# Empty rows written behind the counted tokens, another order in the ramp, operands placed by address modulo 256, and the tokens of expert 1 ahead of its weights' splits

## The chip, the cores and the metric

One core of one Trainium2 chip runs the whole program. The metric is the device time in microseconds (us); a lower time is better. The engines are called as the profile calls them: PE (TensorE, with PEld for its weight loads), DVE (VectorE), ACT (ScalarE), POOL (GpSimd), SP (SyncE, which here only issues DMAs).

## What is computed

Attention with a decaying state feeds a mixture of experts. Shapes: batch 4, 8 heads, 768 steps, head size 48; so 3072 tokens of width 384; 8 experts with 1024 hidden values.

```python
f = 1.0 / (1.0 + np.exp(-f_logit))
for t in range(S):
    state = f[:, :, t, :, None] * state + np.einsum('bhd,bhe->bhde', k[:, :, t], v[:, :, t])
    y[:, :, t] = np.einsum('bhd,bhde->bhe', q[:, :, t], state)
x = y.transpose(0, 2, 1, 3).reshape(B * S, H * D)
logits = x @ w_gate
e_idx = np.argmax(logits, axis=1)          # one expert per token
for e in range(E):
    mask = e_idx == e
    h = np.maximum(x[mask] @ w1[e], 0.0)
    out[mask] = gate_w[mask, None] * eom[mask, e, None] * (h @ w2[e])
```

## The kernel before

**Attention (L131 to L582).** The work is cut into 24 steps t: 4 batches (b) of 6 chunks (c) of 128 tokens. `prep` (L192) makes what step t needs from the raw inputs: `s` and `f` are sigmoids on ACT, `scan_p` and `scan_i` are running products on DVE, `mul_q` multiplies q by p on POOL, `mul_k` multiplies k by i on `eng` (DVE for t below 3 and from 22 on, else POOL, L196), `ends` copies the last column on ACT. The main loop (L462 to L546) calls them two steps ahead through `pre`, which does each only once. On PE a step is `qk(t)` (products of q and k, L249), `kn_tr(t)` (L266), `x_tr(t - 2)` (L326), `out_y(t - 1)` (L309, L313) and `state(t - 1)` (L282). `mask(t, par)` (L252) takes the two halves of the product out of PSUM: one half by an ACT copy and a POOL select, the other by one DVE multiplication; at t = 0 both go by ACT and POOL. `evac_y` (L320) and `evac_kn` are ACT copies that `x_tr` and `state` need.

**Order.** The order in which the program is written is the order on each of PE, ACT, DVE and POOL (`chain`, L1153), so an operation that waits holds everything written behind it on its engine. SP issues DMAs in the written order; eight of its DMAs are in flight, and the ninth waits for the first. `load` (L172) brings q, k, f, v; the loads of batches 2 and 3 are written in the loop at every third step, in the order f, k, q, v (L535).

**Routing.** Every few steps `route` and `slots` count the tokens of each expert; `scatter` (L337) writes each token's row (384 values, token number, logits: 401 values, 1604 bytes) to its slot in `xs_dram`, which has 3072 slots for each of the 8 experts. An expert's matmuls run over a fixed number of slots (`CAPS`: 512, 448, 432, 416, 400, 400, 384, 376, the fullest expert first), so slots behind the last token must hold empty rows with a token number too large to be written out. `clear(e)` (L664), called for all experts ahead of the loop (L434), fills the slots 256 to 511 of every expert with such rows: eight DMAs of 401 KB on SP's queue, behind the loads of batches 0 and 1. The expert with most tokens after step 15 is expert 0 in the order (`top`, L393); its first 256 tokens are read early (`tokens_in`), the rest after the last scatter; `find_order` (L911) then sorts the others.

**Experts (L945 to L1014).** Each value is split into a high and a low part (fp32r), and every product is made of three matmuls. For expert s: `split` cuts the weights (ACT copy, DVE subtraction), `x_in` (L767) turns the tokens by a DVE transpose (`xc`) and splits them (`xh` on ACT, `xl` on DVE), `mm1` (L798) makes 8 blocks f of 9 matmuls into one of two PSUM tiles `h_ps`, which ACT (`hh`, L813) and DVE (`hl`, L814) take out, and then come `mm2` (L828, tokens as the moving operand) for experts 1 to 5 or `mm2_row` (L838, w2 as the moving operand, 384 columns) for experts 0, 6 and 7. Expert 0's first 256 tokens have their own tiles (`xah`, `xal`, and hidden tiles in the pool `ha`), and run through `mm1` before the late tokens arrive; `x_late` (L757) turns the late ones. `gain` steps (L734 to L748, 13 per expert) make the factor of each token. During expert 0's last `mm2_row`s, `beside` (L991) pops at every second call one piece of a list `front` (here: split, tokens 0, split, tokens 1, tokens 2 of expert 1) and at the others one gain step of expert 1.

**Addresses.** A tile's place follows from the sizes allocated ahead of it in its pool. In bytes modulo 256 the program puts `xh`, `xl` and `hh`, `hl` of all late parts at 128, the weights' parts `w1h` to `w2l` at 224, and `xah`, `xal` and the tiles of `ha` at 224.

Of the kernel before, what the change touches and what calls it, by code (L numbers as in the profile page):

```python
# [21 lines left out]
C = 128  # L22
# [26 lines left out]
BW = DM // (128 // SB)  # L49

# [68 lines left out]
class Routing:  # L119


    def __init__(self, pool):
        self.pend = pool.tile([128, NTC * NP], F32, name="pend")

        self.ohb = pool.tile([128, len(RG) + 1, 5, E], BF16, name="ohb")
        self.slot = pool.tile([128, NTC], I32, name="slot")
        self.top = pool.tile([128, E], F32, name="top")
        self.top_id = pool.tile([128, 1], I32, name="top_id")


def attention(ctx, tc, nc, k, kpool, rt, q01, k01, f01, q23, k23, f23, v, wg, xs_dram, r, ex):  # L131
# [60 lines left out]
    def prep(ti):  # L192
# [3 lines left out]
        eng = nc.vector if ti < 3 or ti >= T_VEC else nc.gpsimd  # L196
# [55 lines left out]
    def mask(t, par):  # L252
        if t == 0 or par:
# [83 lines left out]
    def scatter(n):  # L337

        for _ in range(min(n, len(sq))):
# [7 lines left out]
            for other in ex.apart + (ex.cleared if (t + 1) * C <= HELD else []):  # L347
# [56 lines left out]

    def slots(gi, t0, n):
# [8 lines left out]
        if t0 + n == T_TOP:  # L414
            nc.tensor.matmul(cnt_ps, k.ones, r.ohb[:, gi + 1, 0, :], start=True, stop=True, skip_group_check=True)
            top(cnt_ps)
        rk = rt.tile([128, n, E], F32, name="rk")
        nc.vector.tensor_tensor(out=rk, in0=ps, in1=oh, op=ALU.mult)
        with nc.allow_low_precision(reason="one of the summands is not zero"):
            nc.vector.tensor_reduce(out=r.slot[:, ts], in_=rk, axis=AX.X, op=ALU.add)  # L420
        sq.extend(range(t0, t0 + n))
# [11 lines left out]
    for e in range(E):  # L433
        ex.clear(e)  # L434
# [29 lines left out]
    for t in range(last + 1):  # L464
# [6 lines left out]
        if t not in (0, 2):  # L471
# [4 lines left out]
        if t == 2:  # L476
            pre(4, "f")
# [7 lines left out]
        if t > 1 and not late:  # L485
# [18 lines left out]
        pre(t + 2, "mul_q", "ends")  # L504
# [7 lines left out]
        pre(t + 3, "s")  # L512
# [58 lines left out]
    drain()  # L571
    scatter(len(sq))
    ex.tokens_in(0, EARLY // TS, NT)
    ex.mm1_early(3)
    ex.find_order(two[:, 340:340 + E])
# [7 lines left out]
class Experts:  # L583
# [4 lines left out]
    def __init__(self, tc, nc, k, r, raw, right, w1, w2, xs_dram, out, kp, yd):  # L588
        self.tc, self.nc, self.k, self.r, self.raw, self.right, self.kp = tc, nc, k, r, raw, right, kp
        self.yd = yd  # L590
        self.w1, self.w2, self.xs, self.out = w1, w2, xs_dram.rearrange("(e n) w -> e n w", e=E), out
        k.gain = kp.tile([128, SLOTS // SB, E], F32, name="gain")
        k.dst = kp.tile([TS, NT, E], I32, name="dst")
        kp.tile([128, 8], F32, name="pad")

        self.first = kp.tile([TS, NT, RW], F32, name="first_x")
        self.apart, self.cleared, self.results, self.number = [], [], [], {}
        self.wr, self.whl, self.todo, self.gq, self.who = {}, {}, [], [], {}
        self.xg, self.xb, self.xt, self.hs, self.ys, self.ysb = {}, {}, {}, {}, {}, {}
# [11 lines left out]
    def open_rest(self, ctx):  # L611
        pool = lambda name, bufs, **kw: ctx.enter_context(self.tc.tile_pool(name=name, bufs=bufs, **kw))
        self.xp, self.hp, self.yp = pool("mo_x", 2), pool("mo_h", 9), pool("mo_y", 1)
# [50 lines left out]
    def clear(self, e):  # L664

        if e == 0:
            self.empty = self.kp.tile([TS, RW], F32, name="empty")
            self.nc.gpsimd.memset(self.empty, 0.0)
            self.nc.gpsimd.memset(self.empty[:, DM:DM + 1], float(BIG))
        n = (SLOTS - HELD) // TS  # L670
        i = self.nc.sync.dma_start(out=self.xs[e, HELD:SLOTS].rearrange("(j p) w -> p j w", p=TS),
                                   in_=self.empty.unsqueeze(1).broadcast_to([TS, n, RW]))
        self.cleared.append(i)
# [86 lines left out]
    def x_split(self, pool, c, ps, n, width, name):  # L760
        hi = pool.tile([128, width], F32R, name=f"{name}h{c}")
        lo = pool.tile([128, width], F32R, name=f"{name}l{c}")
# [4 lines left out]
    def x_in(self, s, c):  # L767
# [3 lines left out]
        x = self.xp.tile([128, SLOTS], F32, name="xc")  # L771
        self.nc.vector.transpose(out=x[:, 0:n].rearrange("p (a t) -> p a t", t=SB), in_=t[:, :, c::KC])
        self.xt[s, c] = self.x_split(self.xp, c, x[:, 0:CAPS[s]], CAPS[s], WIDE, "x")
# [459 lines left out]
```

## Time and profile before

| | us |
|---|---|
| median of 3 runs | 358.79 (358.48 to 359.13) |
| the profiled execution | 361.26 |
| its span (first to last instruction) | 359.6 |
| PE busy | 344.4 (96%) |
| DVE busy | 260.7 (73%) |
| ACT busy | 183.3 (51%) |
| POOL busy | 144.4 (40%) |

The span is one execution under the profiler, 1.66 us shorter than that execution's own time, and the execution is 2.47 us longer than the median of the runs without a profile. Busy time of PE contains overlapping matmuls, so PE's losses are read from the start times of its matmuls and from the idle time in square brackets that the timeline puts behind an instruction, with what ended it.

### The profile page before, as it was taken

To read this page: it belongs to the slowest core of one execution; us is meant where nothing else is said; L and a number is where in the kernel's file an instruction comes from. 1 tells how busy PE (TensorE), PEld (TensorE's weight loads), DVE (VectorE), ACT (ScalarE), POOL (GpSimd) and SP (SyncE) were. 2 spreads that over 40 slices of the span, in tenths; PEclk is the share of its full clock that TensorE was granted. 3 is DMA by queue.
4 is the path that set the end of the run, shared out by engine and by line. 5 is a ranking of instruction groups with operands and counts; after the bars stand their busy time and mean duration, and the time that the engine had idled before them with its cause. 6 is when DMAs were issued, how large, how long until landed. Compare 5 with 4: busy or idle time off the path is not lost. (4 is left out here: it accounts for less than half of the span.)

```text
span 359.6 us, 8283 instructions
## 1 busy us (share of the span) xinstructions
PE 344.4 (96%) x3001; PEld 317.9 (88%) x3001; DVE 260.7 (73%) x519; ACT 183.3 (51%) x436; POOL 144.4 (40%) x174
## 2 busy tenths in 40 slices
PE   7899999999999999999999999999999999999994
PEld 2678898888888799997999899999999999999993
DVE  6998988888998566576685884975975974966510
ACT  3476776766675743455542453452552552464510
POOL 7586786999988753022000005005005005007112
PEclk9999999999999999999999999999999999999998
DMA  7999999999746614999458298398598299292101
GB/s 258 349 360 354 342 257 244 244 264 258 248 128 231 251 48 136 223 281 242 128 168 136 50 324 252 57 313 256 81 311 261 63 300 273 62 288 81 42 24 43
DMA packets 81458, 74.02 MB, mean 206 GB/s; under 512 B 37058, under 2 KB 76037, under 8 KB 81408
## 3 DMA queue, kind: packets, MB, share of 16 engines
q1 hardware_dynamic: 78096, 63.76, 64.6%
q0 software_dynamic: 3312, 9.65, 7.7%
q8 instruction: 25, 0.41, 0.5%
q14 instruction: 25, 0.20, 0.2%
HBM read 57.16 MB, written 16.68 MB: 205 GB/s over the span
## 5 line engine op out<-in xcount | busy, mean ns | idle before, releaser
L888 POOL DMA_INDIRECT out<-yr,dst x20 | 22.1, 1107 | 134.2 <-DMA yr<-yd 88.6
L813 ACT ACTIVATE hh<-h_ps 128x256 fp32r<-128x256 f32 (+6 forms) x72 | 34.9, 484 | 67.2 <-PE h_ps L809 58.7
L809 PE MATMUL h_ps<-xh,w1h 128*128 128x400 f32 (+6 forms) x192 | 66.9, 348 | 0.9 <-DVE hl L814 0.7
L814 DVE SCALAR_TENSOR_TENSOR hl<-h_ps,hh 128x256 fp32r<-128x256 f32 (+6 forms) x72 | 38.8, 539 | 38.2 <-ACT hh L813 34.9
L809 PE MATMUL h_ps<-xl,w1h 128*128 128x400 f32 (+6 forms) x192 | 65.1, 339 | 0.2 <-DVE xl L764 0.2
L809 PE MATMUL h_ps<-xh,w1l 128*128 128x400 f32 (+6 forms) x192 | 65.0, 338 | 0.0
L828 PE MATMUL y_ps<-hh,w2h 128*128 128x400 f32 (+3 forms) x120 | 42.2, 352 | 0.0
L828 PE MATMUL y_ps<-hh,w2l 128*128 128x400 f32 (+3 forms) x120 | 42.1, 351 | 0.0
L828 PE MATMUL y_ps<-hl,w2h 128*128 128x400 f32 (+3 forms) x120 | 42.1, 351 | 0.0
L809 PEld LDWEIGHTS h_ps<-xh,w1h 128*128 128x128 f32 x192 | 36.0, 188 | 6.3 <-DVE hl L814 4.7
L809 PEld LDWEIGHTS h_ps<-xl,w1h 128*128 128x128 f32 x192 | 36.1, 188 | 0.9 <-DVE xl L764 0.5
L809 PEld LDWEIGHTS h_ps<-xh,w1l 128*128 128x128 f32 x192 | 36.0, 188 | 0.5
L227 POOL TENSOR_TENSOR q_t<-q_t,p 128x512 f32<-128x512 f32 x24 | 30.6, 1273 | 9.0 <-DVE p L213 5.7
L653 DVE TENSOR_TENSOR w2l<-w2r,w2h 128x768 fp32r<-128x768 f32 x31 | 30.6, 988 | 3.4 <-ACT w2h L652 1.5
L249 PE MATMUL a_ps<-q_t,k_t 64*128 64x128 f32 x384 | 28.4, 285 | 3.5 <-DVE k_t L224 2.6
L213 DVE TENSOR_TENSOR_SCAN p<-f_ps,start_p 128x511 f32<-128x511 f32 x22 | 28.0, 1274 | 4.7 <-ACT f_ps L208 2.3
L653 DVE TENSOR_TENSOR w1l<-w1r,w1h 128x768 fp32r<-128x768 f32 x28 | 26.8, 957 | 3.5 <-ACT w1h L652 2.7
L249 PEld LDWEIGHTS a_ps<-q_t,k_t 64*128 64x128 f32 x384 | 23.7, 187 | 6.1 <-POOL q_t L227 1.9
L326 PE MATMUL x_ps<-turn,xt 128*128 128x112 f32 x192 | 26.0, 278 | 1.8 <-ACT xt L320 1.7
L220 DVE TENSOR_TENSOR_SCAN i<-f_ps,start_i 128x512 f32<-128x512 f32 x22 | 26.9, 1223 | 0.8
L343 POOL DMA_INDIRECT xs_dram<-xn,slot x24 | 24.2, 1010 | 7.7 <-issue 3.8
L838 PE MATMUL y_ps<-w2h,hh 128*128 128x384 f32 (+1 forms) x80 | 27.1, 339 | 0.0
(175 smaller groups left out, 764.7 us busy)
## 6 DMA issues: line engine op xcount, KB each, us to landing
w1r<-in_w SPq DMA_DIRECT2D x32, 384.0 KB
w2r<-in_w SPq DMA_DIRECT2D x32, 384.0 KB
xs_dram<-empty SPq DMA_DIRECT2D x8, 401.0 KB
f_t<-in_f SPq DMA_DIRECT2D x6, 512.0 KB
q_t<-in_q SPq DMA_DIRECT2D x6, 512.0 KB
k_t<-in_k SPq DMA_DIRECT2D x6, 512.0 KB
v_t<-in_v SPq DMA_DIRECT2D x6, 512.0 KB
v_t<-in_v SPq DMA_DIRECT2D x4, 768.0 KB
```

What stands on the lines that cost most here:

```text
L213: nc.vector.tensor_tensor_scan(out=flat(d["p"])[:, 1:n], data0=flat(d["f"])[:, 0:n - 1], data1=sp[:, 1:n], initial=sp[:, 0:1], op0=ALU.mul ...
L220: nc.vector.tensor_tensor_scan(out=flat(d["i"])[:, ::-1], data0=flat(d["f"])[:, ::-1], data1=flat(k.start_i[z])[:, ::-1], initial=0.0, op0 ...
L227: nc.gpsimd.tensor_tensor(out=q_t[i][:, :, sl], in0=q_t[i][:, :, sl], in1=d["p"], op=ALU.mult)
L249: nc.tensor.matmul(aps[t][par][:, g, :], k_t[b % 2][r, g, sl], q_t[b % 2][r, g, sl], start=(g == 0), stop=(g == NP - 1))
L326: nc.tensor.matmul(xps[t][:, g, :], xt[t][:, g, :], turn[:, g, :], start=(g == 0), stop=(g == NP - 1))
L343: i = nc.gpsimd.indirect_dma_start(out=xs_dram, out_offset=bass.IndirectOffsetOnAxis(ap=r.slot[:, t:t + 1], axis=0), in_=xn[t // 4][:, t % ...
L653: (eng or self.nc.vector).tensor_tensor(out=flat(lo), in0=raw, in1=flat(hi.bitcast(F32)), op=ALU.subtract)
L809: nc.tensor.matmul(ps[:, 0:n], a[:, c, cs], b, start=(i == 0), stop=(i == 3 * KC - 1))
L813: nc.scalar.activation(out=hi, in_=ps[:, 0:n], func=AF.Relu)
L814: nc.vector.scalar_tensor_tensor(out=lo, in0=ps[:, 0:n], scalar=0.0, in1=hi.bitcast(F32), op0=ALU.max, op1=ALU.subtract)
L828: self.nc.tensor.matmul(self.yps[d][:, 0:n], a[:, d, fs], b, start=(f == 0 and i == 0), stop=(f == KF - 1 and i == 2), skip_group_check=True)
L838: self.nc.tensor.matmul(ps[0:n, 0:DM], a, b[:, f % 2, :], start=(f == 0 and i == 0), stop=(f == KF - 1 and i == 2))
```

## The change

1. **Empty rows.** The eight early DMAs go. `empty_rows` only makes the empty tile. A new `clear(s, start)` loads a row number into SP's register and writes 256 empty rows (128 for experts 6 and 7) from that row on, behind the counted tokens. For expert 0 the row comes from five new small DVE operations (`behind`) after the last `slots`, and the DMA stands ahead of the last scatters and of the read of the late tokens; for expert 1 it comes from three new DVE operations in `find_order` and stands ahead of the load of its w1; for expert s + 1 it stands ahead of the load of its w1, in expert s. One matmul of the counts moves from `find_order` to the last `slots`.
2. **Ramp.** `mul_k(0)` goes from DVE to POOL; `mul_q` and `ends` are written ahead of `scan_i` for steps 0 and 1; `s` and `f` of steps 2, 3 and 4 are written earlier; `ends` and `scan_i` of step 3 are written one step later, behind `evac_y(0)`; step 1's mask goes by ACT and POOL in both halves.
3. **Load order** of batches 2 and 3: f, q, k instead of f, k, q.
4. **Addresses.** Pads of 48, 48, 16 and 16 values and offsets `X_AT`, `H_AT` inside the tiles. With the new small tiles the pad in the constants moves everything behind it by 256 bytes, so what stays without an offset keeps its address modulo 256. With the offsets (8 values are 32 bytes, 24 are 96) the tokens' parts of experts 4, 5 and 6 and the hidden parts of 4 and 5 start at 224, like the weights; the tokens' and hidden parts of expert 0 (late) and the hidden parts of 6 and 7 start at 160; `xah`, `xal` and the tiles of `ha` move from 224 to 160.
5. **Expert 1.** Its tokens' transposes and splits stand ahead of its last two weight splits, and its gain steps move from expert 0's `mm2_row`s into its own `mm1`, two per block.

```diff
+X_AT = (8, 0, 0, 0, 24, 24, 24, 0)
+H_AT = (8, 0, 0, 0, 24, 24, 8, 8)
...
-        eng = nc.vector if ti < 3 or ti >= T_VEC else nc.gpsimd
+        eng = nc.vector if ti in (1, 2) or ti >= T_VEC else nc.gpsimd
...
-        if t == 0 or par:
+        if t < 2 or par:
...
+    def behind(ps):
+        nc.vector.tensor_copy(out=r.behind, in_=ps)
+        at, one = rt.tile([128, E], F32, name="key"), rt.tile([128, 1], F32, name="mx")
+        nc.vector.tensor_tensor(out=at, in0=r.top, in1=r.behind, op=ALU.mult)
+        nc.vector.tensor_reduce(out=one, in_=at, axis=AX.X, op=ALU.add)
+        nc.vector.tensor_scalar(out=r.top_row, in0=one, scalar1=float(E * N - SLOTS), scalar2=None, op0=ALU.min)
...
-    for e in range(E):
-        ex.clear(e)
+    ex.empty_rows()
...
-    for names in (("f", "s"), ("scan_p", "scan_i", "mul_k", "mul_q", "ends")):
+    for names in (("f", "s"), ("scan_p", "mul_q", "ends", "scan_i", "mul_k")):
         pre(0, *names)
         pre(1, *names)
+    pre(2, "s", "f")
...
-        if t not in (0, 2):
+        if t > 3:
             pre(t + 2, "f")
...
         if t == 2:
-            pre(4, "f")
+            pre(3, "ends", "scan_i")
+        if t == 3:
+            pre(5, "f")
...
-        if t == 0:
-            pre(2, "s", "f")
+        if t in (1, 2):
+            pre(t + 2, "s", "f")
...
-        pre(t + 2, "scan_p", "scan_i")
+        pre(t + 2, "scan_p")
+        if t != 1:
+            pre(t + 2, "scan_i")
...
-            load(b + 2, [("fkq", c, c + 3)])
+            load(b + 2, [("fqk", c, c + 3)])
...
     drain()
+    ex.apart.append(ex.clear(0, r.top_row[0:1, 0:1]))
     scatter(len(sq))
     ex.tokens_in(0, EARLY // TS, NT)
...
+    def clear(self, s, start):
+        n = len(self.rows(s)) * TS - HELD
+        row = self.nc.values_load(start, engines=[mybir.EngineType.SP], min_val=0, max_val=E * N - n)
+        i = self.nc.sync.dma_start(
+            out=self.all_rows[bass.ds(row, n)].rearrange("(j p) w -> p j w", j=2),
+            in_=self.empty[0:n // 2].unsqueeze(1).broadcast_to([n // 2, 2, RW]))
...
             lambda: tt(out=k.perm, in0=by_e(at), in1=k.place, op=ALU.is_equal),
+            lambda: tt(out=cube, in0=k.perm, in1=by_e(r.behind), op=ALU.mult),
+            lambda: red(out=at, in_=cube, axis=AX.X, op=ALU.add),
+            lambda: nc.vector.tensor_scalar(out=k.row, in0=at, scalar1=float(E * N - SLOTS), scalar2=None, op0=ALU.min),
+            lambda: self.clear(1, k.row[0:1, 1:2]),
...
             if s > 0 and s + 1 < E:
+                self.clear(s + 1, self.k.row[0:1, s + 1:s + 2])
                 self.load(s + 1, self.k.number[0:1, s + 1:s + 2], rest=False)
...
-                if s == 0:
+                if s < 2:
                     self.gain(2)
...
+            if s == 0:
+                front[:0] = [lambda f=f, c=c: f(1, c) for f, c in (
+                    (self.x_turn, 0), (self.x_turn, 1), (self.x_cut, 0), (self.x_turn, 2), (self.x_cut, 1), (self.x_cut, 2))]
...
-                    else:
+                    elif s > 0:
                         self.gain(1)
```

## Rows read from the trace of the kernel before

**Rows 1.** The page: busy time, and the DMA engines' share over 40 slices.

```profile
PE 344.4 (96%) x3001; PEld 317.9 (88%) x3001; DVE 260.7 (73%) x519; ACT 183.3 (51%) x436; POOL 144.4 (40%) x174
DMA  7999999999746614999458298398598299292101
```

**Rows 2.** Timeline of PE, the ramp: start, us, engine, line, operation, [idle before].

```profile
9.24 1.16 PE L249 MATMUL a_ps<-q_t,k_t 64*128 64x128 f32 x16 [1.44 <-DVE k_t L224]
...
19.27 1.15 PE L326 MATMUL x_ps<-turn,xt 128*128 128x112 f32 x8 [0.60 <-ACT xt L320]
...
24.46 1.15 PE L326 MATMUL x_ps<-turn,xt 128*128 128x112 f32 x8 [0.29 <-ACT xt L320]
```

**Rows 3.** Timelines of DVE and ACT in the same stretch, same columns.

```profile
8.44 0.69 DVE L224 TENSOR_TENSOR k_t<-k_t,i 128x512 f32<-128x512 f32 x1
...
18.09 0.20 ACT L230 COPY pend<-p 128x4 f32<-128x4 f32 x1 [1.91 <-DVE p L213]
```

**Rows 4.** Timeline of SP's queue, the early writes of empty rows.

```profile
32.61 7.76 SPq L671 DMA_DIRECT2D xs_dram<-empty  x8
42.14 1.29 SPq L189 DMA_DIRECT2D f_t<-in_f  x2
```

**Rows 5.** Timelines of PE, and one row of POOL, from 54 to 73 us.

```profile
56.36 1.15 PE L326 MATMUL x_ps<-turn,xt 128*128 128x112 f32 x8 [0.20 <-ACT xt L320]
...
64.88 1.23 PE L249 MATMUL a_ps<-q_t,k_t 64*128 64x128 f32 x16 [0.60 <-POOL k_t L224]
...
72.71 0.44 PE L313 MATMUL two_ps<-at,v_t 128*64 128x128 f32 x4 [0.90 <-DMA v_t<-in_v]
...
61.00 1.28 POOL L227 TENSOR_TENSOR q_t<-q_t,p 128x512 f32<-128x512 f32 x1 [3.13 <-DVE misc L296]
```

**Rows 6.** Windows: us; busy of PE, PEld, DVE, ACT, POOL; PE clock; DMA; GB/s.

```profile
74.20:101.20 27.00, 26.82 (x433) 24.05 (x431) 24.24 (x48) 19.29 (x60) 25.39 (x27) 1.00 0.92 239
```

**Rows 7.** Timelines of PE and DVE where expert 1 begins.

```profile
163.11 0.37 PE L809 MATMUL h_ps<-xh,w1h 128*128 128x448 f32 x1
...
168.06 0.47 PE L809 MATMUL h_ps<-xh,w1h 128*128 128x448 f32 x1 [0.33 <-DVE hl L814]
168.37 0.36 PE L809 MATMUL h_ps<-xl,w1h 128*128 128x448 f32 x1
...
168.97 0.36 PE L809 MATMUL h_ps<-xl,w1h 128*128 128x448 f32 x1
...
167.39 0.62 DVE L814 SCALAR_TENSOR_TENSOR hl<-h_ps,hh 128x448 fp32r<-128x448 f32 x1
```

**Rows 8.** Timelines of DVE, POOL and SP between last count and expert 1's loads.

```profile
130.94 0.17 DVE L420 TENSOR_REDUCE slot<-rk 128x2 int32<-128x16 f32 x1
...
140.06 0.17 DVE L935 CAST number<-o_at 128x8 int32<-128x8 f32 x1
...
135.07 0.98 POOL L343 DMA_INDIRECT xs_dram<-xn,slot  x1 [0.30 <-issue]
...
137.89 0.37 SPq L678 DMA_DIRECT2D first_x<-xs_dram  x1
141.06 3.02 SPq L622 DMA_DIRECT2D w1r<-in_w  x4
```

**Rows 9.** Timeline of PE: first and last of three runs of like matmuls.

```profile
136.26 0.34 PE L838 MATMUL y_ps<-w2h,hh 128*128 128x384 f32 x1
...
142.51 0.38 PE L757 MATMUL x_ps<-ident,first_x 128*128 128x128 f32 x2
...
155.17 0.34 PE L838 MATMUL y_ps<-w2h,hh 128*128 128x384 f32 x1
...
162.94 0.33 PE L838 MATMUL y_ps<-w2l,hh 128*128 128x384 f32 x1
...
263.00 0.35 PE L828 MATMUL y_ps<-hh,w2h 128*128 128x400 f32 x1
...
275.97 0.34 PE L828 MATMUL y_ps<-hl,w2h 128*128 128x400 f32 x1
```

More of the change, by code (lines that the diff above doesn't have):

```diff
@@ L128, in __init__ @@
         self.top_id = pool.tile([128, 1], I32, name="top_id")
+        self.top_row = pool.tile([128, 1], I32, name="top_row")
+        self.behind = pool.tile([128, E], F32, name="behind")
 def attention(ctx, tc, nc, k, kpool, rt, q01, k01, f01, q23, k23, f23, v, wg, xs_dram, r, ex):
@@ L345, in scatter @@
                 in_=xn[t // 4][:, t % 4, :], in_offset=None, bounds_check=E * N - 1, oob_is_err=False)
-            for other in ex.apart + (ex.cleared if (t + 1) * C <= HELD else []):
+            for other in ex.apart:
                 tc.declare_no_dep(i.ins, other.ins, reason="other slots")
@@ L416, in slots @@
             top(cnt_ps)
+        if t0 + n == NTC:
+            nc.tensor.matmul(cnt_ps, k.ones, r.ohb[:, gi + 1, 0, :], start=True, stop=True, skip_group_check=True)
         rk = rt.tile([128, n, E], F32, name="rk")
@@ L484, in attention @@
         fill(more)
-        if t > 1 and not late:
+        if t > 2 and not late:
             pre(t + 2, "scan_p")
@@ L503, in attention @@
         evac_kn(t)
-        pre(t + 2, "mul_q", "ends")
+        pre(t + 2, "mul_q")
+        if t != 1:
+            pre(t + 2, "ends")
         if hot(t - 2):
@@ L574, in attention @@
     ex.mm1_early(3)
-    ex.find_order(two[:, 340:340 + E])
+    ex.find_order()
     for f in range(4, KF):
@@ L612, in open_rest @@
         pool = lambda name, bufs, **kw: ctx.enter_context(self.tc.tile_pool(name=name, bufs=bufs, **kw))
+        self.wp.tile([128, 48], F32, name="w_pad", bufs=1)
+        self.ha.tile([128, 16], F32, name="ha_pad", bufs=1)
         self.xp, self.hp, self.yp = pool("mo_x", 2), pool("mo_h", 9), pool("mo_y", 1)
@@ L662, in rows, with empty_rows @@
         return [(j, min(TS, CAPS[s] - j * TS)) for j in range(NT) if CAPS[s] > j * TS]
[L664 to L673, printed above, removed]
+    def empty_rows(self):
+        self.empty = self.kp.tile([TS, RW], F32, name="empty")
+        self.nc.gpsimd.memset(self.empty, 0.0)
+        self.nc.gpsimd.memset(self.empty[:, DM:DM + 1], float(BIG))
+    def clear(self, s, start):
[4 more added lines that the diff above has]
+            in_=self.empty[0:n // 2].unsqueeze(1).broadcast_to([n // 2, 2, RW]))
+        for other in self.apart:
+            self.tc.declare_no_dep(i.ins, other.ins, reason="rows behind the tokens")
+        return i
     def tokens_in(self, s, j0, j1):
@@ L783, in x_early @@
             self.xt["early", c] = self.x_split(self.xa, c, at[c], EARLY, EARLY, "xa")
+        self.xa.tile([128, 16], F32, name="xa_pad")
     def x_late(self):
@@ L810, in mm1 @@
                 i += 1
-        pool, width = (self.ha, EARLY) if early else (self.hp, WIDE)
-        hi, lo = (pool.tile([128, width], F32R, name=m)[:, 0:n] for m in ("hh", "hl"))
+        pool, width, at = (self.ha, EARLY, 0) if early else (self.hp, WIDE, H_AT[s])
+        hi, lo = (pool.tile([128, width], F32R, name=m)[:, at:at + n] for m in ("hh", "hl"))
         nc.scalar.activation(out=hi, in_=ps[:, 0:n], func=AF.Relu)
@@ L922, in find_order @@
         by_e = lambda a: a.unsqueeze(1).broadcast_to([128, E, E])
-        nc.tensor.matmul(ps, k.ones, r.ohb[:, len(RG), 0, :], start=True, stop=True, skip_group_check=True)
-        nc.vector.tensor_tensor(out=cnt, in0=ps, in1=k.slot0, op=ALU.subtract)
+        k.row = kp.tile([128, E], I32, name="row")
+        nc.vector.tensor_tensor(out=cnt, in0=r.behind, in1=k.slot0, op=ALU.subtract)
         self.todo += [
@@ L979, in run @@
                      if (1, s + 1, i) in self.wr]
-            for c in range(KC):
-                front.insert(2 * c + 2 if s > 0 else 2 * c + 1, lambda c=c: self.x_in(s + 1, c))
+            if s == 0:
+                front[:0] = [lambda f=f, c=c: f(1, c) for f, c in (
+                    (self.x_turn, 0), (self.x_turn, 1), (self.x_cut, 0), (self.x_turn, 2), (self.x_cut, 1), (self.x_cut, 2))]
+            else:
+                for c in range(KC):
+                    front.insert(2 * c + 2, lambda c=c: self.x_in(s + 1, c))
             if s + 1 == E:
```

41 lines of the change are left out of this document (25 added, 16 removed).

## The prediction

> **What bounds the kernel now.** I read the page's busy times first, then PE's timeline from end to end, then the timelines of whatever engine stands in the brackets of PE's idle rows. PE is busy 96% of the span, and no other engine comes near [rows 1]. So a change is worth what it takes out of PE's own stream: idle time in front of a matmul, or the spacing of matmuls that follow each other without a wait. Everything behind PE's last matmul (one ACT copy, one scatter, its landing) stays as it is. PE loses time in four places that this change touches. In the ramp, its first product of q and k comes at 9.24 after 1.44 us idle, and `x_tr(0)` and `x_tr(1)` wait 0.60 and 0.29 us for ACT's copies [rows 2]. Between 56 and 73 us it waits 0.20, 0.60 and 0.90 us [rows 5]. Where expert 1 begins it stumbles [rows 7]. And like matmuls are not equally fast [rows 9].
>
> **Part A, the ramp.** `mul_k(0)` moves from DVE (0.69 us from 8.44 [rows 3]) to POOL, where a product of that shape takes 1.28 us [rows 5]. It starts at about the same time, so the first `qk` comes some 0.6 us later, at about 9.85. In exchange DVE is free 0.6 us earlier for step 1, and since PE has the four warm-up matmuls to do in between, the second `qk` comes no later than before. The gain lies at `x_tr(0)`: ACT stands 1.91 us idle until 18.09 for `ends(3)`, which waits for `scan_p(3)` on DVE, and `evac_y(0)` is queued behind it [rows 3]. That is why PE starts `x_tr(0)` only at 19.27. In the new order `ends(3)` stands behind `evac_y(0)`. Laying the old durations out in the new order, I get `qk(2)` at about 15.8, `evac_y(0)` at 16.5 to 17.2 and `x_tr(0)` at 17.5, 1.8 us earlier. At `x_tr(1)` the copy is again late (ACT has `evac_x` and the sigmoids of step 5 ahead of it): I get 23.1 against 24.46 [rows 2], 1.3 us earlier. From step 4 on DVE and ACT are ahead of PE again, and 1.2 us remain. Bounds: 0.3, where only the bracket of row 24.46 goes, and 2.2, where both late copies go and nothing new comes. Value taken: 1.2.
>
> **Part B, the queue of loads.** The eight early writes are issued from 32.61 on; the next load, the ninth, must wait for the first of them and is issued at 42.14, so such a write takes 9.5 us to land there [rows 4], in slices where the DMA engines are 9 tenths busy [rows 1]. So the loads of batches 2 and 3 come some 9 us later than without the writes. All three waits of [rows 5] are of that kind. The 0.90 names the load of v. The 0.60 names `mul_k(12)`, and that is late since POOL had stood idle for 3.13 us in front of `mul_q(12)`: the releaser named there is not an operand of that instruction, and p was long ready, so it was the load of q. The 0.20 is a copy behind a sigmoid that waited for f. With the loads 9 us earlier all go: 0.20 + 0.60 + 0.90 = 1.70 us. The order f, q, k helps the same wait again and is worth nothing once it is gone. What is late next is POOL: where nothing waits, it is busy 25.39 of 27.00 us while PE is busy 26.82 [rows 6]. It keeps up there, so I let it keep up here too. Bounds 0.9 (only the wait that names a load) and 2.1 (the brackets leave out the first matmuls' longer spacing). Taken: 1.7.
>
> **Part C, expert 1.** From 163.11 to 168.37 stand 19 steps from matmul to matmul, and three steps behind them take 0.60 us, so 0.20 each [rows 7]. The 19 took 5.26 instead of 3.80: 1.46 us are lost. The first part is `xl`, which comes late because splits of w1 and gain steps are in front of it; the second is `hl` of block 0, which DVE starts only at 167.39 behind seven gain steps, while PE waits for its PSUM tile [rows 7]. In the new order the tokens' transposes and splits come ahead of the weights' splits and the gain steps are out of the way. The price is two gain steps of 0.2 to 0.8 us beside each block of expert 1's `mm1`, where a block takes nine times 0.20 = 1.80 us of PE, `hl` 0.62 us of DVE and every second block a split of about 0.95. Sum on DVE for two blocks: about 3.2 of 3.6 us. That fits, with a small wait or two. Bounds 0.5 and 1.46; taken: 1.25.
>
> **Part D, the addresses.** The same `mm2_row` matmul runs at two rates. From 136.26 to 142.51 stand 36 of them, 173.6 ns each; there the stationary operand (from `ha`) and the moving one (w2) both lie at 224 modulo 256. From 155.17 to 162.94 stand 44 steps, 176.6 ns each; there the stationary operand lies at 128 [rows 9]. The 400-column matmuls of expert 4 take (275.97 - 263.00) / 71 = 182.7 ns [rows 9], with moving at 128 and stationary at 224. [...] The `mm2_row`s of late expert 0, 6 and 7 go from 128 to 160 for the stationary operand: 192 x 3.0 = 0.6 us at best. The early 48 go from 224 to 160: 48 x 3.0 = 0.15 us lost at worst. No row shows 160. Bounds -0.3 (both new places bad) and 1.3; taken 0.6, near the middle, as half of the matmuls go to a pairing that a row shows to be the faster one. [...]
>
> **Part E, what is added.** For expert 0 the row number needs five small DVE operations behind 130.94 (0.17 us each by that row, with gaps about 1 us), which fall into time in which DVE waits for ACT. SP then loads the number and issues the write at about 133, while the last scatter is issued at 135.07 and the read of the late tokens waits for it until 137.89 [rows 8]. The new write hides beside the scatters if it lands within some 4.7 us. The read of as many rows does: it is issued at 137.89, and PE turns the tokens at 142.51 [rows 9] without a wait, 4.6 us later. For expert 1 three more operations delay the number from 140.06 [rows 8] by 0.7 us, and the second write waits until the late tokens have been read, so that SP's load of w1 moves from 141.06 to about 142.7 and the tokens' blocks behind it by as much. They are used from about 156 on, with three more us until PE needs the first. For the later experts the write stands ahead of loads that SP issues a whole expert early. Cost taken: nothing; bounds 0 and 1.5.
>
> **Sum.** 1.2 + 1.7 + 1.25 + 0.6 = 4.75 us of PE's stream. Against the profiled execution's own 361.26: 356.5. The median of the runs lies 2.47 us below that execution, and I carry this difference over: 358.79 - 4.75 = 354.0. Its own range: 352.4 to 355.6. All bounds at their good end give 0.3 less than 352.0 (7.06 us gained); all at the bad end, with 1.5 for E, about 358.6.
>
> **The rivals.**
> - *Placement gives nothing.* The rates depend on how the streams happen to meet, not on addresses. For it: within one expert the same form changes rate without a change of address. Against: the two blocks of [rows 9] each hold their rate for 36 and 44 matmuls. Time: 358.79 - 4.15 = 354.6.
> - *POOL becomes the bound.* With PE's waits gone, POOL's 94% of [rows 6] is what PE meets, and half of A and B comes back as waits for `mul_k`: 358.79 - 3.3 = 355.5. Against: in that window PE ran without waits beside it.
> - *The ramp gains nothing*, since DVE's running products and the later first product set it: 358.79 - 3.55 = 355.2.
> - *The late writes are slow* (slower than before). If a write behind the counts takes the 9.5 us of [rows 4], it lands at about 142.6, the late tokens are read 4.7 us later than now, and PE stands still at `x_late` for 3.4 us (4.7 less some slack ahead of 142.51, which no row shows); the second write waits for that, its own 9.5 us pass before the blocks of expert 1 can be read, and PE waits about 3 to 4 us again where expert 1 begins, where C's gain is lost too. Then -4.75 + 1.25 + 3.4 + 3.5 = +3.4, 362.2. It starts to cost at a landing over 5 to 6 us and makes the whole slower than before over about 8. Against it: in the two slices around 135 (126 to 144 us) the DMA engines are 1 and 4 tenths busy, not 9 [rows 1].
>
> **Chances.** Forecast 0.50; placement nothing 0.16; POOL 0.10; ramp nothing 0.08; slow writes 0.07; all parts near their good ends (about 352.0) 0.07; no net difference because several bad ends meet (358.6) 0.02. A difference below 0.2% can't be told from none here. Faster: 0.91; same: 0.02; slower: 0.07. The range that leaves out the slow writes, the meeting of bad ends and the outer end of the good ones: 351.9 to 356.6.
>
> **What would show it.** A: `x_tr(0)` without a wait near 17.5 and `qk(3)` 1 to 2 us earlier, the first `qk` 0.6 us later. B: no write of empty rows before 130, none of the three brackets. C: matmuls of expert 1 every 0.20 us from the first on. D: `mm2_row` of 6 and 7 at 173 to 174 ns and 400 columns at 180. E: the read of late tokens still released by a scatter, not by the write. The prediction is wrong if PE waits ahead of `x_late`, if the brackets of [rows 5] come back with POOL's name, or if the spacing of like matmuls rises.

## The result, and the profile after

The changed kernel has a median of 356.17 us (six runs, 354.42 to 357.65); the kernel before 359.19 (six runs, 358.48 to 361.0; three of them are those of its table above, the other three have a median of 360.49). The ratio is 0.9891 with a 95% interval of 0.9862 to 0.9921: between 2.8 and 5.0 us less. In a later session it was 356.27 beside 360.31, ratio 0.9899 (0.9868 to 0.9930). The forecast was 4.75 us less and 354.0. The profiled execution took 357.65 us with a span of 355.8, 3.7 us under the span of before (355.85 and 359.55 before rounding).

The first two lines are the page's busy times, the third its DMA share over 40 slices; they answer to [rows 1].

```profile
PE 343.3 (96%) x3001; PEld 316.5 (89%) x3001; DVE 260.1 (73%) x524; ACT 183.5 (52%) x437; POOL 146.6 (41%) x176
DMA  7999999998146624989777399399599399282101
```

PE is still the bound. The loads end in slice 10 and not in slice 11. The ramp, in PE's timeline of the changed kernel (start, us, engine, line, operation, [idle before and what ended it]):

```profile
9.85 1.16 PE L253 MATMUL a_ps<-q_t,k_t 64*128 64x128 f32 x16 [0.91 <-POOL k_t L228]
...
17.31 1.04 PE L330 MATMUL x_ps<-turn,xt 128*128 128x112 f32 x8
...
22.20 1.15 PE L330 MATMUL x_ps<-turn,xt 128*128 128x112 f32 x8
```

Against [rows 2] the first product is 0.61 us later, the two `x_tr` are 1.96 and 2.26 us earlier and their waits are gone. The same view from 54 to 83 us, beside [rows 5]:

```profile
56.36 0.27 PE L317 MATMUL two_ps<-at,v_t 128*64 128x128 f32 x1 [0.33 <-issue]
...
62.36 1.16 PE L253 MATMUL a_ps<-q_t,k_t 64*128 64x128 f32 x16
...
64.27 1.15 PE L330 MATMUL x_ps<-turn,xt 128*128 128x112 f32 x8 [0.17 <-ACT at L258]
...
69.53 0.44 PE L317 MATMUL two_ps<-at,v_t 128*64 128x128 f32 x4
...
73.61 0.47 PE L330 MATMUL x_ps<-turn,xt 128*128 128x112 f32 x2 [0.20 <-issue]
...
81.98 0.19 PE L422 MATMUL two_ps<-ohb,upper 128*128 128x32 bf16 x1 [1.19 <-issue]
```

The two long brackets of [rows 5] (`qk` at 62.36, the first use of v at 69.53) are gone. In their place PE stands idle four times, three of them with "issue" behind the arrow: it waits for nothing that the profile shows. The matmul at 81.98 had no wait in the kernel before. SP's queue and PE around the late tokens, beside [rows 8, 9]:

```profile
130.63 0.41 SPq L699 DMA_DIRECT2D xs_dram<-empty  x1
135.82 0.39 SPq L709 DMA_DIRECT2D first_x<-xs_dram  x1
139.22 0.40 SPq L699 DMA_DIRECT2D xs_dram<-empty  x1
...
140.47 0.38 PE L788 MATMUL x_ps<-ident,first_x 128*128 128x128 f32 x2
```

The late write landed at 133.54 (2.91 us), the last scatter at 135.81, so the scatter releases the read of the late tokens, as before; the read landed at 139.21, and PE turned the tokens 1.26 us later without a wait. The start of expert 1 on PE, ACT and DVE, beside [rows 7]:

```profile
160.85 0.37 PE L848 MATMUL h_ps<-xh,w1h 128*128 128x448 f32 x1
...
165.04 0.47 PE L848 MATMUL h_ps<-xh,w1h 128*128 128x448 f32 x1 [0.41 <-DVE hl L853]
...
163.31 0.58 ACT L882 ACTIVATE o<-y_ps,gain 128x384 f32<-128x384 f32 x1 [3.46 <-DMA out<-o,dst]
163.79 0.54 ACT L852 ACTIVATE hh<-h_ps 128x448 fp32r<-128x448 f32 x1
...
164.36 0.62 DVE L853 SCALAR_TENSOR_TENSOR hl<-h_ps,hh 128x448 fp32r<-128x448 f32 x1 [3.38 <-ACT hh L852]
```

The wait for `xl` is gone, one for `hl` is left. And two runs of like matmuls, first and last, beside [rows 9]:

```profile
152.52 0.33 PE L877 MATMUL y_ps<-w2h,hh 128*128 128x384 f32 x1
...
160.67 0.34 PE L877 MATMUL y_ps<-w2l,hh 128*128 128x384 f32 x1
...
259.84 0.34 PE L867 MATMUL y_ps<-hh,w2h 128*128 128x400 f32 x1
...
272.62 0.34 PE L867 MATMUL y_ps<-hl,w2h 128*128 128x400 f32 x1
```

47 steps of the first take 173.4 ns each (176.6 before), 71 of the second 180.0 (182.7 before). Laying the starts of the same matmuls in the two traces side by side gives where the 3.7 us of span come from:

```
stretch of before                  us      forecast
ramp, to 28 us                   -2.15     A  -1.2
the three brackets of [rows 5]   -2.03     B  -1.7
four new waits, 56 to 82 us      +2.60     none
one wait of before at 111 gone   -0.75     none
rest of 28 to 125 us             +0.36
125 to 163 us                    -0.29     (part of D)
expert 1's mm1                   -0.75     C  -1.25
mm1/mm2 of experts 4 to 7, rest  -1.08     D  -0.6
behind PE's last matmul          +0.42     none
```

### The profile page after: what moved, and what is told of

Same layout as the page of the kernel before. It is cut to its first block, busy times and chain, and to the rows that moved or that the text cites. A ratio compares the mean times of both kernels' runs of the same rounds, so it can differ in the third digit from the quotient of the medians.

```text
span 355.8 us, 8327 instructions
## 1 busy us (share of the span) xinstructions
PE 343.3 (96%) x3001; PEld 316.5 (89%) x3001; DVE 260.1 (73%) x524; ACT 183.5 (52%) x437; POOL 146.6 (41%) x176
## 5 line engine op out<-in xcount | busy, mean ns | idle before, releaser
L945 POOL DMA_INDIRECT out<-o,dst x10 | 10.8, 1078 | 40.3 <-ACT o L882 21.0
```

## Experiments

**Are A and B two separate gains?** Two kernels take one part each into the kernel before. The first has only the ramp's order:

```diff
-        eng = nc.vector if ti < 3 or ti >= T_VEC else nc.gpsimd
+        eng = nc.vector if ti in (1, 2) or ti >= T_VEC else nc.gpsimd
...
-    for names in (("f", "s"), ("scan_p", "scan_i", "mul_k", "mul_q", "ends")):
+    for names in (("f", "s"), ("scan_p", "mul_q", "ends", "scan_i", "mul_k")):
```

> The kernel before with part A alone (order of the ramp); everything else as before, addresses too. Theory 'parts add': what the ramp gains at 28 us (2.15 us in the trace of the changed kernel) reaches the end, so about 357.1 where the kernel before runs at 359.2. Theory 'the loads take it back': the loads of batches 2 and 3 still stand behind the eight early writes, which do not come earlier when PE does; then the three waits of before near 56, 65 and 73 us grow from 0.20 + 0.60 + 0.90 by nearly the 2.15 us, the starts behind 75 us lie only 0 to 0.7 us ahead of before, and the time is 358.5 to 359.2.

360.63 us beside 360.11, ratio 1.0004 (0.9982 to 1.0027): alone the ramp gives nothing. At 30 us PE was 2.17 us ahead of before, as in the changed kernel. Then one row of PE's timeline:

```profile
56.18 1.98 PE L326 MATMUL x_ps<-turn,xt 128*128 128x112 f32 x8 [2.19 <-ACT xt L320]
```

and three windows (us; busy of PE, PEld, DVE, ACT, POOL; clock; DMA; GB/s):

```profile
55.00:57.00 2.00, 0.82 (x4) 0.82 (x5) 1.57 (x4) 2.00 (x6) 0.83 (x2) 0.82 1.11 278
57.00:59.00 2.00, 2.00 (x22) 1.62 (x21) 1.97 (x4) 1.01 (x6) 0.33 (x1) 0.50 1.13 260
59.00:61.00 2.00, 2.00 (x40) 1.79 (x36) 1.35 (x6) 0.18 (x2) 1.26 (x2) 0.82 1.04 306
```

The bracket that was 0.20 at 56.36 is 2.19: the load of f comes when it came before, and the whole ramp's gain is waited away at this one place. Worse, behind this one long wait the granted clock was 0.50 from 57 to 59 us (1.00 in the trace of before), and the matmuls up to 60 us took 1.55 us more (PE from 0.17 ahead of before to 1.38 behind). The ten runs of this kernel have a median mean clock of 0.993 (0.992 to 0.996), those of before 0.997 (0.991 to 1.000), which suggests that most of them pay for that; one trace shows it. The second kernel has only the late empty rows and the order f, q, k:

```diff
-    for e in range(E):
-        ex.clear(e)
+    ex.empty_rows()
...
+    ex.apart.append(ex.clear(0, r.top_row[0:1, 0:1]))
...
-            load(b + 2, [("fkq", c, c + 3)])
+            load(b + 2, [("fqk", c, c + 3)])
```

> The kernel before with parts B and E alone (empty rows written late, loads in the order f, q, k); ramp, addresses and expert 1 as before. Theory 'parts add': the three waits go, 1.7 to 2.1 us less, about 357.3 where the kernel before runs at 359.2, and no wait of POOL's name between 54 and 84 us. Rival 'PE's own instructions': idle times of PE that nothing in the profile explains (issue) appear between 54 and 115 us, 0.3 to 1.3 us each, at places 256 instructions of PE apart, just behind the 16 KB packets of an instruction queue, and leave 0.5 to 1.5 us of the gain. Rival 'late writes cost': PE waits ahead of the late tokens' transposes near 142 us.

360.62 us beside 360.11, ratio 1.0012 (0.9990 to 1.0035): nothing either. The three brackets are gone and PE is 1.99 us ahead at 72.7, but then:

```profile
82.58 0.20 PE L284 MATMUL one_ps<-v_t,kn 128*64 128x48 f32 x1 [1.06 <-issue]
```

1.26 us of it went back here, one matmul ahead of the matmul of the counts where the changed kernel stands. No wait had POOL's name. Expert 1 then took back another 0.35 us in `mm1` and 0.46 in `mm2`, expert 2 0.16 in `mm1`, and not by waits: nearly all of expert 1's matmuls of 448 columns came every 206.7 ns. In each of the other 13 traces they come every 200.0, also in that of the same kernel with halved loads (rows_half below), whose operands have the same addresses. First and last of 54 such matmuls of `mm2`, here and there:

```profile
178.17 0.37 PE L847 MATMUL y_ps<-hh,w2h 128*128 128x448 f32 x1
...
189.12 0.36 PE L847 MATMUL y_ps<-hl,w2h 128*128 128x448 f32 x1
```

```profile
177.62 0.36 PE L847 MATMUL y_ps<-hh,w2h 128*128 128x448 f32 x1
...
188.22 0.36 PE L847 MATMUL y_ps<-hl,w2h 128*128 128x448 f32 x1
```

The granted clock was 1.00 in this stretch; what else made them slower is not shown. So the parts don't add: A needs B's early loads, and what B frees meets a stall that no step of mine had.

**What is that stall?** The records of the DMA queues hold 25 packets of 16 KB on the queue that the page calls q8 instruction. PE runs 6074 instructions (3001 matmuls, 3001 weight loads and 72 of its sequencer), so one packet for some 243 of them. In the changed kernel PE's "issue" waits stand at instructions 1473, 1985 and 2241 of its stream (to within two places, in the order of their starts), whole multiples of 256 apart. My estimate from the two counts and this spacing is that one packet brings about 256 of PE's instructions; the page does not say which engine q8 serves. Call a place where by this estimate a new block of 256 begins an edge. Worked out from the records of three traces ("halves" is the kernel with halved loads, below; the instruction at an edge is the one that stands there, where one does):

```
              packet starts, us after the     packet has landed, us before
              previous edge of 256            the instruction at the edge
edge          before  changed  halves         before  changed  halves
1217           2.72    5.06     0.35           4.30    1.76     6.07
1473           3.93    5.93     1.08           3.61    1.57     5.70
1729           3.78    5.49     3.44           3.39    1.31     2.87
1985           4.67    6.77     1.39           4.14    1.50     6.18
2241           3.38    5.54     0.72           2.30    1.62     5.05
```

Where PE stood at an edge, 0.17 us or more, the packet had landed only 1.3 to 1.6 us earlier; where it had landed over 2 us earlier, PE ran through. In the kernel with the empty rows alone the wait of 1.06 us, at another operation, is at instruction 2241 too: its stream has one more instruction ahead of that place. Three runs test the reading. The same kernel once more:

> The changed kernel once more, for a second trace. In its first trace PE stands without a named releaser at instructions 1473, 1985 and 2241 of its stream (matmuls and weight loads counted together), 256 or twice that apart, each time 1.5 to 1.6 us after a 16 KB packet of its instruction queue has landed. Theory 'PE's own instructions come late': stalls only at 1473, 1729, 1985 or 2241 again, in other sizes, always 1.3 to 1.6 us behind a packet, and the times spread over 3 us as they did (354.4 to 357.7). Rival 'a hidden wait of the program': the same three stalls with the same 0.5, 0.5 and 1.3 us.

356.27 us (355.43 to 358.51). PE stood in front of 1217, 1473, 1729 and 2241, always 1.3 to 1.8 us behind a packet, but with other sizes: the steps there are 0.36, 0.33, 0.99 and 0.18 us (for the third the profile names a copy of ACT). The 1.19 us of the first trace were one draw of many. One with 44 more instructions in the warm-up:

```diff
-    warm_up(nc, k, ps, WARM)
+    for _ in range(2 * WARM):
+        nc.tensor.matmul(ps[:, 0:256], k.warm[:, 0:128], k.warm[:, 0:256], start=True, stop=True)
```

> The changed kernel with the 22 matmuls of the warm-up ahead of the first step cut into 44 of half the columns: 44 more instructions in PE's stream, no other work, and they end before the first product is due. Theory 'PE's own instructions come late': the late edges stay at 1473, 1729, 1985, 2241 of the stream as counted, which is 44 instructions earlier in the program, so the stall of 1.19 us is no longer at the matmul of the counts (line of slots) but some 22 matmuls ahead of it. Rival 'a hidden wait of the program': the stall stays at that matmul, now number 2285.

357.24 us (355.91 to 358.80). The matmul of the counts has no wait now; PE stands at 1217 and 1473 of the stream as counted, at other places of the program:

```profile
46.95 0.44 PE L318 MATMUL two_ps<-at,v_t 128*64 128x128 f32 x4 [0.21 <-issue]
...
55.34 0.48 PE L331 MATMUL x_ps<-turn,xt 128*128 128x112 f32 x3 [0.43 <-issue]
...
80.55 0.19 PE L423 MATMUL two_ps<-ohb,upper 128*128 128x32 bf16 x1
```

So in these runs the stall goes with the number of the instruction, not with the operation. At 2241, some 22 matmuls ahead of the counts, I had expected the long wait; PE doesn't stand there in this trace, where the packet landed 1.6 us ahead. And one where the loads of batches 2 and 3 are cut in halves:

```diff
-                    nc.sync.dma_start(out=t[64 * par:64 * par + D, :, sl],
-                                      in_=rest[b - 2, par::2, :, sl].rearrange("g d s -> d g s"))
+                    for g in (slice(0, 2), slice(2, 4)):
+                        nc.sync.dma_start(out=t[64 * par:64 * par + D, g, sl],
+                                          in_=rest[b - 2, par::2, :, sl][g].rearrange("g d s -> d g s"))
```

> The changed kernel, each load of q, k and f of batches 2 and 3 cut into two of half the size, so that the eight DMAs in flight hold about half the bytes. Theory 'the backlog of loads delays PE's instructions': packets of the instruction queue start 2 to 4 us after the previous edge of 256 instructions in place of 5.1 to 6.8, the stalls at 1473, 1985 and 2241 go, 1 to 2 us less than the changed kernel (about 354.7 where that has a median of 356.2) and a narrower spread. Rival 'the engines are full either way': packets start as late as now and the stalls stay; same time. Rival 'SP is the bound': loads arrive later, and waits on f, q or v come back ahead of steps 12 to 18, 0.2 to 2 us.

354.84 us (354.16 to 355.91) beside 356.27 of the changed kernel and 360.31 of before; ratio to before 0.9845 (0.9823 to 0.9867). The windows from 45 to 85 us, first of the changed kernel, then of this one:

```profile
45.00:85.00 40.00, 37.94 (x596) 33.41 (x599) 33.76 (x65) 26.78 (x83) 34.23 (x36) 1.00 1.09 249
```

```profile
45.00:85.00 40.00, 39.82 (x642) 35.72 (x642) 36.26 (x71) 28.98 (x89) 36.40 (x38) 1.00 1.02 272
```

PE is busy 39.82 of 40 us and not 37.94, the packets start 0.4 to 3.4 us after the previous edge and not 5.1 to 6.8 (table above), no "issue" wait is left there, and between 24 and 81 us PE gains 2.90 us on the changed kernel's trace. POOL is busy 91% of this stretch without being waited for. The loads in flight, not any engine, were what B's faster queue met. Why smaller DMAs let the packet through earlier is not shown.

**Expert 1.** The chain of the profile after is: `o` waits for a scatter, `hh` is queued behind `o` on ACT, `hl` waits for `hh`, PE for `hl`. A fourth buffer takes the first link away:

```diff
-        t = self.yp.tile([TS, DM], F32, name="o", bufs=3)
+        t = self.yp.tile([TS, DM], F32, name="o", bufs=4)
```

> The changed kernel with a fourth buffer for the result rows o. Theory: the one wait that is left at expert 1's start (0.41 us for hl) is a chain: the third buffer's scatter lands at 163.21, ACT's copy into o waits for it until 163.31, block 0's hh stands behind that copy on ACT, hl behind hh. With four buffers the copy runs near 161, hh near 162.8, and matmuls of expert 1 come every 0.20 us from the first on: 0.6 us less than the changed kernel (355.6 where that runs at 356.2). Rival: the two gain steps beside each block and the splits make hl late (my price in part C); then the wait stays and the time is the changed kernel's.

356.90 us (354.36 to 359.05), no different from the changed kernel's 356.2 within this spread; but the trace shows the mechanism:

```profile
159.58 0.58 ACT L882 ACTIVATE o<-y_ps,gain 128x384 f32<-128x384 f32 x1 [1.19 <-PE y_ps L877]
161.40 0.55 ACT L852 ACTIVATE hh<-h_ps 128x448 fp32r<-128x448 f32 x1 [1.24 <-PE h_ps L848]
```

Both copies now wait for PE alone, and 72 matmuls of `mm1` take 200.3 ns each without a wait: 14.42 us from the first to the next stage, against 15.11 in the changed kernel's trace and 15.86 before. In the second trace of the changed kernel it is 14.5 with three buffers, in that of the halves 14.4: PE came there at another moment against the scatters. So C is worth 0.75 to 1.46 us, by when the scatters land, and the gain steps cost nothing.

**Addresses.** The changed kernel with other offsets:

```diff
-X_AT = (8, 0, 0, 0, 24, 24, 24, 0)
-H_AT = (8, 0, 0, 0, 24, 24, 8, 8)
+X_AT = (0, 0, 0, 0, 48, 32, 56, 16)
+H_AT = (0, 0, 0, 0, 40, 16, 48, 56)
```

> The changed kernel with other offsets: tokens' parts of experts 4, 5, 6, 7 at 64, 0, 96, 192 modulo 256, hidden parts at 32, 192, 64, 96, late expert 0 at 128 as in the kernel before; weights stay at 224. Like matmuls of before and after: 176.7 ns (hidden stationary at 128) against 173.4 (at 224 or 160) for 384 columns, 182.7 (moving at 128) against 180.0 (at 224) for 400. Theory 'only 128 is bad': all eight new places run at the lower figure, expert 0's late rows at 176.7 again. Theory 'multiples of 64 are bad': 64, 0 and 192 run at the higher figure, 32 and 96 at the lower one. Theory 'must be 224 or 160, as the weights': all at the higher figure. Theory 'placement is nothing': late expert 0 stays at 173.4.

355.47 us in one run. First and last of three runs of like matmuls: late expert 0 (stationary at 128), expert 4's `mm2` (moving at 32), expert 5's (moving at 192):

```profile
149.69 0.34 PE L877 MATMUL y_ps<-w2h,hh 128*128 128x384 f32 x1
...
157.99 0.34 PE L877 MATMUL y_ps<-w2l,hh 128*128 128x384 f32 x1
...
257.20 0.34 PE L867 MATMUL y_ps<-hh,w2h 128*128 128x400 f32 x1
...
269.98 0.34 PE L867 MATMUL y_ps<-hl,w2h 128*128 128x400 f32 x1
...
283.75 0.34 PE L867 MATMUL y_ps<-hh,w2h 128*128 128x400 f32 x1
...
296.76 0.34 PE L867 MATMUL y_ps<-hl,w2h 128*128 128x400 f32 x1
```

47 steps of 176.6 ns, 71 of 180.0, 71 of 183.2. All places against weights at 224, median step where a stage has waits:

```
400 columns, moving at        0: 180   32: 180.0   64: 185   128: 182.7   192: 183.2   224: 180.0
384 columns, stationary at   64: 173.4   96: 175.7   128: 176.6   160: 173.4   224: 173.4
384 columns, moving at       96: 175   224: 173;     376 columns, moving at  128: 171.8   192: 173.2
```

Going back to 128 brings the old rate back, and the rates of 384 and 400 columns are the same in every trace with the same places (`mm2_row` of expert 6 at 176.7 ns and `mm2` of experts 4 and 5 at 182.2 to 182.7 in the four with 128, 173.3 and 180.0 in the nine with the new places), so for these forms placement it is. But none of my three rules holds: 64 is the worst place for a moving operand and a good one for a stationary one, 32 is good and 96 is not. Which pairs are good was found here by trying; the rule stays open. With 416, 432 and 448 columns, tried at 128 alone, nothing is lost in most traces: they take 186.7, 193.3 and 200.0 ns, each 16 columns 6.7 ns more from 180.0 for 400 on. Placement isn't all, though: in two traces one such form ran 6.7 ns slower at the same addresses, 448 columns at 206.7 (the empty rows alone) and 432 at 200.0 in `mm2` of expert 2 (the next experiment).

**A slow late write.** The write for expert 0 issued three times, each behind the last:

```diff
-    ex.apart.append(ex.clear(0, r.top_row[0:1, 0:1]))
+    for again in range(3):
+        ex.apart.append(ex.clear(0, r.top_row[0:1, 0:1], again))
...
-        for other in self.apart:
+        for other in self.apart[:-1] if again else self.apart:
```

> The changed kernel with expert 0's late write of empty rows issued three times in a row, each waiting for the one before: the last lands some 8.7 us after the first is issued at 130.6 (one took 2.91). My rival of slow writes: the read of the late tokens waits for it (139.3 in place of 135.8), PE stands at the late transposes for the 3.5 us less 1.26 us of slack (the read landed at 139.21, the first transpose ran at 140.47), 2.2 us; the write and loads of expert 1 go out 3.5 us later and PE stands 0 to 3 us at expert 1's start; whole 358.4 to 361.4. Rival 'hidden further': PE finds no wait, since the rows of expert 0 that are early give it enough work; whole as the changed kernel.

362.82 us in one run beside 360.31 of before. SP's queue and PE:

```profile
129.28 7.04 SPq L700 DMA_DIRECT2D xs_dram<-empty  x3
140.13 0.40 SPq L710 DMA_DIRECT2D first_x<-xs_dram  x1
...
143.41 0.69 PE L789 MATMUL x_ps<-ident,first_x 128*128 128x128 f32 x2 [4.14 <-DMA first_x<-xs_dram]
```

and windows, columns as above:

```profile
139.00:143.00 4.00, 0.27 (x2) 0.00 (x0) 0.00 (x0) 0.00 (x0) 0.00 (x0) 0.82 0.41 122
143.00:145.00 2.00, 1.59 (x7) 1.60 (x8) 0.00 (x0) 0.11 (x1) 0.26 (x1) 0.50 0.95 304
145.00:147.00 2.00, 2.00 (x8) 2.00 (x8) 1.18 (x3) 0.91 (x3) 0.00 (x0) 0.50 0.96 304
```

The third write landed at 140.02, 10.7 us after the first was issued (3.0, 3.6 and 4.1 us), later than the 8.7 that I had reckoned. PE stood 4.14 us, and then its clock was at 0.50 for some four more: the matmuls of 384 columns came every 0.32 us, another 2.3 us. Expert 1 had no further wait; expert 2's `mm2` lost 0.5 us by the slower rate just named. The rival's mechanism is real, and its price here 6.5 us over the changed kernel; the single write of 2.91 us stays clear of it.

**Combinations.** The part B/E kernel from above with halved loads:

> The kernel before with the late empty rows and the order f, q, k alone, and the loads in halves. With whole loads this part alone gave nothing (360.62 beside 360.11), though the three waits were gone (1.99 us at 72.7) and 1.26 us of it came back as a stall at instruction 2241. Theory 'the gain was there and was lost to PE's late instructions': with halves the stall is gone and the part is worth 1 to 2 us, 358.2 to 359.2 beside 360.2. Rival 'it is lost at expert 1': PE waits for xl and hl where expert 1 begins as in the kernel before or longer, and the time stays near 360.

360.55 us (359.90 to 360.76) beside 360.17, ratio 1.0007 (0.9995 to 1.0019). Between 45 and 85 us PE is busy 39.82 us and 38.12 in the trace of before, and it is 2.25 us ahead at 72 to 110 us. Two other "issue" waits then cost 0.31 and 0.54 us more than in that trace (109.5, 133.7; neither is at an edge), expert 1 loses its 1.46 us as before, and the stretch behind PE's last matmul is 0.69 us longer. That leaves 0.7 us against the trace of before, which took 361.26 where runs of before beside this kernel have a median of 360.17. So B alone gives nothing that the runs show, with halves too; which waits in the trace of before are not in its usual execution stays open. The halves with four result buffers, the same with 26 warm-up matmuls, and the same with the order f, k, q:

```diff
-WARM = 22
+WARM = 26
...
-            load(b + 2, [("fqk", c, c + 3)])
+            load(b + 2, [("fkq", c, c + 3)])
```

> The changed kernel with the loads of q, k and f of batches 2 and 3 in halves and a fourth buffer for the result rows: both remedies together. Theory 'they are separate stalls': 0.3 to 0.7 us less than the halves alone (354.84), about 354.3, no stall at PE's edges of 256 instructions from 1217 to 2241 and matmuls of expert 1 every 0.20 us from the first on. Rival 'the fourth buffer only moves the wait': the time of the halves alone.

> The same with 26 in place of 22 warm-up matmuls. In the trace of the halves the warm-up ended at 7.6 us, PE stood 2.16 us until the first product at 9.96, and the granted clock was 0.50 from 12 to 14 us, so PE came 1.6 us later out of the ramp than in the changed kernel's trace (warm-up to 8.9, idle 0.91, clock 1.00). Theory 'the later first product leaves PE idle long enough to lose its clock in some executions': with the warm-up until 8.5 or later no execution loses it, and the median is 0 to 1 us under that with 22, about 353.8. Rival 'it was one execution under the profiler': same median.

> The kernel with halves and four buffers, loads of batches 2 and 3 in the order f, k, q of the kernel before. Theory (my prediction): once the loads come 9 us earlier the order is worth nothing; same time as with f, q, k (about 354.3), no wait of POOL's name ahead of steps 12 to 18. Rival: q is late again, and a wait for mul_k of 0.2 to 0.6 us comes back near 63 us.

355.21 us (354.68 to 356.96), 355.01 (354.88 to 355.94) and 354.99 (354.51 to 356.59), beside 360.17: no two differ within this spread. The order f, k, q costs nothing and brings no wait of POOL's name. The fourth buffer adds nothing that can be measured; in all three traces PE loses about 0.9 us at 107 us instead. That is at instructions 3111 to 3127 of the stream, between the edges 3009 and 3265, and the trace of before loses 0.75 us at nearly the same matmuls (111 us), so this is another stall; its cause is open. On the warm-up the runs are inconclusive: the two runs over 356 us of the first kernel have a mean clock of 0.991 and 0.992, the others 0.996 to 0.998, and with 26 the one run over 355.2 has 0.993. The halves alone (354.84, in an earlier session) are the lowest median, and none of the three is told from them.

## Why the prediction was right or wrong, by its steps

- **The total.** Faster, and inside the range, but near its upper end: 3.0 us by the first medians and 4.0 by the later ones, for 4.75. The sum came out near only because terms missed in both directions, so part of that is luck. The bad ends of all bounds add up to 1.4 us gained and 1.5 lost, 358.9 and not 358.6.
- **A, 1.2 us.** The steps held to 0.2 us: first `qk` 9.85 (forecast 9.85), `qk(2)` 15.72 (15.8), `x_tr(0)` 17.31 (17.5). Only `x_tr(1)` came 0.9 earlier than laid out, so A gave 2.15, the upper bound. What failed is that the term stood by itself in the sum: alone it is waited away at the next load (2.19 us at 56.18).
- **B, 1.7 us.** The three waits went, 2.03 us, and the order of q and k was worth nothing, as said. The step that failed is "what is late next is POOL". By the reading above it was PE's own instructions: 2.60 us in the first trace, about 1.4 in the medians (356.27 against 354.84 with halves). I had priced the loads by who waits for their data, and not by what else travels on the same DMA engines (q8's packets, 0.5% of the 16 engines' span by the page of the changed kernel); the 9 tenths of [rows 1] were in view.
- **A and B together** are what forecast and runs agree on, if instructions come in time: before less halves is 5.47 us; less 1.30 for D and 1.46 for C leaves 2.7, for 2.9 in the sum. That is a subtraction of figures read from traces: no run has A and B without C and D. That the two alone give nothing (part B even with halves) is only half explained.
- **C, 1.25 us.** Mechanism right, 0.75 to 1.46 measured. The "small wait or two" came, but not from the gain steps: from a result buffer three steps up on ACT, which neither the price nor the bounds named.
- **D, 0.6 us.** Mis-sized to its good bound: 1.30, added up from the stages whose spacing fell. Its good bound of 1.3 has 0.7 us for the 400 columns of experts 4 and 5, a term that no run shows; the traces of before and after show 0.57 there (`mm2` 0.19 less in each, at 180.0 ns for 182.7, `mm1` 0.10 and 0.09 less). 160 is as good as 224, and the 48 early matmuls lost nothing (173.4 ns). I took the middle for want of a row on 160. The rival "placement gives nothing" is out as a forecast, but another rate without another address was seen beside placement: 206.7 against 200.0 ns for one form. Why one form takes 176.6 ns with the stationary operand at 128 and 173.4 at 160 is not shown, nor where in PE the time is lost.
- **E, nothing.** Right up to PE's last matmul: the scatter releases the read, no wait at `x_late`. "Everything behind PE's last matmul stays as it is" was not: from its last start to the end it is 5.68 us before, 5.80 with the ramp alone and 6.0 to 6.4 in all twelve traces with late writes. Why is not shown.
- **The offset.** I carried the 2.47 us between the profiled execution and the median of before over to the sum. After has 1.48 there, and later medians of before are 360.1 to 360.3. A bracket in a trace that lies above the median may be part of what lifts it there.

## What to carry to other kernels

A wait that goes away is worth its length only if nothing else is due at the same moment: before adding up gains of consecutive stages, ask for each whether it survives with the others undone, and try the parts alone. When transfers are made to run ahead, look at what shares the DMA engines with them, an engine's own instructions included (here, by my reading, 25 packets of 16 KB); where idle time says "issue", count the instructions between two such places. Cutting loads into smaller DMAs was worth more here (356.27 to 354.84 us) than any further reordering.

## What the runs showed of the hardware that I had not expected

- PE's instructions seem to arrive in packets of 16 KB, one per about 256: an estimate from q8's 25 packets beside 6074 instructions and from waits at 1473, 1985 and 2241. In the changed kernel, with whole loads of q, k and f, the packet started 5.1 to 6.8 us after the previous edge, with halves 0.4 to 3.4, and at the edges from 1217 to 2241 PE stood, 0.2 to 1.3 us, only where it landed less than 1.8 us ahead of the instruction.
- One idle stretch of 2.2 us (56 us, ramp alone) and one of 4.1 (x_late, three writes) were each followed by a granted clock of 0.50 and cost 1.5 and 2.3 us more than the wait itself. In the ramp of the halves it was the same, after 2.16 us ahead of the first product (window, columns as above):

```profile
12.00:14.00 2.00, 2.00 (x8) 0.78 (x8) 1.93 (x3) 0.93 (x3) 1.85 (x3) 0.50 1.14 328
```

Idle stretches of 1.69 to 1.80 us at that place in four other traces (1.69 with the empty rows alone, 1.77 with the ramp alone) left the clock there at 1.00.

- The step of like matmuls went with the pair of places, modulo 256, of moving and stationary operand: with weights at 224, 173.4 to 176.6 ns for 384 columns and 180 to 185 for 400. For 416, 432 and 448 columns, at 128 alone, it was 186.7, 193.3 and 200.0 ns in most traces. And one form at the same addresses ran at two rates in two executions: 200.0 and 206.7 ns for 448 columns, 193.3 and 200.0 for 432, at a granted clock of 1.00.
